# Sparse attention and a ReLU-squared layer: the scores of a batch's two local pairs as one group of 24 matmuls in six PSUM banks

## The chip, the cores and the metric

The kernel runs on one core of a Trainium2 chip. The metric is device time in microseconds (us) of one execution; a figure without further words is the median of several. One execution was also taken by the profiler, and its times are the ones that the lines of the profile show. The engines are named as in the profile: PE (TensorE, matmuls) with PEld (its weight loads), ACT (ScalarE), DVE (VectorE), POOL (GpSimd) and SP (SyncE, here a queue of DMA starts). Each engine takes its instructions in the order in which the program gives them.

## What is computed

Attention with two sparse masks over 8 batches, 8 heads, 576 positions of 64 values, then a two-layer network over the 4608 tokens:

```python
mask_local = (rel >= 0) & (rel < 32)                       # heads 0 to 3
mask_strided = (rel >= 0) & (pos[None, :] % 32 == pos[:, None] % 32)   # heads 4 to 7
attn = softmax(where(mask, q @ k.T / sqrt(64), -1e9))
x = (attn @ v)            # to [8*576, 8*64] = [4608, 512]
h = x @ w_in              # 512 -> 2048
out = relu(h)**2 @ w_out  # 2048 -> 512
```

Inputs and output are float32; the kernel computes with bfloat16 operands.

## The kernel before

**Units.** Heads go in pairs, since two heads of 64 values fill 128 partitions: unit u = 4 b + p is pair p of batch b. Pairs 0 and 1 of a batch are local, pairs 2 and 3 strided. A local query sees only the 31 positions before it, so the scores of a local unit are cut into six blocks of 96 queries against 128 keys. Each block is one matmul per head (line 493): 64 rows of the array, weights from `kT`, moving data from `qT`, 96 columns. The first head of the pair lies in partitions 0 to 63 and the second in 64 to 127 (`row` 0 and 1 in the code), and the matmuls of the two alternate.

**Groups.** The network is the main line of work. It is cut into chunks of 512 tokens (c = 0 to 8). Each chunk has 16 groups of the first layer (line 662: four matmuls of 512 columns into a `ph` bank, then a ReLU on ACT, line 668, then its square on DVE, line 669) and 16 groups of the second layer (line 684: four matmuls; after each fourth group a copy on ACT, line 688, and a store). That gives 288 groups, numbered 0 to 287: group n belongs to chunk n // 32 and is of the first layer where n % 32 < 16. `ph` has two banks, used in turn.

**The plan.** The attention of the batches after the first is woven into these groups by a hand-written table, `PLAN`: "44: S9! D8.0" means that before group 44 the steps S of unit 9 and D of unit 8 are issued. The letters that matter here: T transposes q or k of a unit on PE; S makes the scores of a unit; D (lines 614 to 628) multiplies the exponentials of one head (`.0` or `.1`) with v, six matmuls of 65 columns, and DVE normalises the result; E sends it, by a transposing DMA on SP's queue, to `xt`, the input of the network; Q, C, U and V start loads on POOL's queue; X and Y start transposing DMAs on SP's; s and x are the two halves of the strided pairs' attention; k, B and c are copies that prepare operands.

**Step S from batch 1 on.** It takes four banks from the ring `pt`, two per head, and puts three blocks (288 columns) into each. ACT then takes the exponential of each bank (line 503), and DVE multiplies with the 0/1 mask (line 509), one instruction of 576 columns per head. With "!" the four exponentials are issued at once and the masks of the two heads one and two ticks later; without it the exponentials too are spread over ticks. A tick follows each group: work that was put off with `later(n, ...)` is issued at the n-th tick from there. The square of a group's ReLU is put off by one, so it is issued right behind its own group.

**Banks.** PSUM has eight: two `ph`, five `pt`, one `py`. `bank("pt")` hands out the banks of the ring in order, so each step gets the one that was used longest ago. `py` is last used in chunk 0, that is, before group 32. Step x (lines 544 to 568) takes two banks: `pn` for the sums and `po` for the result; ACT takes the logarithm of `pn` (line 554) and the exponential of that (line 555), and only then DVE multiplies `po` with it into `xt` (line 562, six instructions of 144 columns; for part 2 line 568, four instructions), so `po` stays in use until the last of these.

Of the kernel before, what the change touches and what calls it, by code (L numbers as in the profile page):

```python
# [9 lines left out]
BF16 = mybir.dt.bfloat16  # L10
AF = mybir.ActivationFunctionType
ALU = mybir.AluOpType
# [42 lines left out]
38: T8qv C3k  # L55
39: k20v
40: U3
41: S8! k21v
42: T9qa
44: S9! D8.0  # L60
46: D8.1
47: E8
48: D9.0 Q16k s2.0
49: s2.1
50: Q17q Q16q s2.2 c12kv
51: D9.1 c12qa
52: Q17k c13kv c13qa
54: x2.0 X3q
55: E9 X3k C4k C4q
56: x2.1  # L70
57: T12ka
58: V4 T13qv T12qa
59: T13ka
60: x2.2 B30v
61: B31v
63: U4 S12!
64: X4q
65: D12.0
66: Y17 k30v
67: Y16 D12.1 S13! X4k C5q k31v  # L80
68: C5k
71: s3.0 E12 Q20k Q21q Q20q
72: Q21k s3.1
# [5 lines left out]
83: x3.1  # L89
89: x3.2  # L90
90: k40v
91: S16! k41v
95: U5 D16.0 D16.1
96: S17
97: Y20
99: X5k
100: C6k
# [11 lines left out]
114: k51v  # L109
116: x4.0  # L110
119: x4.1
124: V6
125: x4.2
128: U6 S20!
130: S21
133: D20.0
134: Y24 D20.1 X6k
135: E20 X6q s5.0 C7q Q28k
# [8 lines left out]
150: x5.1 k60v  # L127
152: k61v
153: x5.2
155: S24!  # L130
156: V7
157: U7
161: S25
162: D24.0
165: s6.0 D24.1
166: s6.1
# [7 lines left out]
179: s6.2  # L144
182: x6.1
186: x6.2
188: k70v
189: k71v
191: S28!
192: S29  # L150
197: s7.0
198: D28.0 s7.1
199: D29.0
# [10 lines left out]
def kernel(  # L164
# [9 lines left out]
    nc = tc.nc  # L174
# [40 lines left out]
    def bank(nm):  # L215
        if in_b0[0] and nm == "pt":
            nm = "b0"
        t = banks[nm].pop(0)
        banks[nm].append(t)
        while id(t) in unread:  # L220
            run_due(lambda x: x[1] == unread[id(t)])
        return t
# [16 lines left out]
    mask_bd = singles.tile([128, 1, W3], BF16)  # L239
    str_rows_t = {nm: singles.tile([SR, RW], BF16, name=f"{nm}_t") for nm in "qk"}  # L240
    kTl = [singles.tile([128, 32 + S], BF16, name=f"kTl{i}") for i in range(NV)]
    es = [singles.tile([128, 1280], BF16, name=f"e{i}") for i in range(4)]
    xt = [singles.tile([128, T], BF16, name=f"xt{p}") for p in range(4)]
    w_in_b = singles.tile([128, 4, d_ff], BF16)
    w_out_b = singles.tile([128, 16, d_model], BF16)
# [188 lines left out]
    def later(n, fn, key=None):  # L434
        pending.append((clock[0] + n, key, fn))

    def run_due(test):
        due = [x for x in pending if test(x)]
        for x in due:
            pending.remove(x)  # L440
        for x in sorted(due, key=lambda x: x[0]):
            x[2]()
# [23 lines left out]
    def step_S(u, mode=0):  # L466
        s = st[u]
        qT, kT = s["qT"], s["kT"]
        local = is_local(u)
        w, n = (QL, NL) if local else (SP_, NJ)  # L470
        kn = 128 if local else SP_
        hn = n // 2
        e = es[u % 4]
        s["e"] = e
        pss = [[None, None], [None, None]]
        for half in range(2):
            for row in range(2):
                pss[row][half] = bank("pt")
                if u < 4:
                    bias = bias_l[:, half].rearrange("p t c -> p (t c)") if local \  # L480
                        else bias_s.rearrange("p t c -> p (t c)")
                    nc.tensor.matmul(pss[row][half][0:kn, 0:S // 2], ident[0:kn, 0:kn], bias,
                                     start=True, stop=False, skip_group_check=True)
            for i in range(hn):
                t = half * hn + i
                klo = w * t
                for row in range(2):
                    rows = slice(64 * row, 64 * row + 64)
                    if not local:
                        lhsT, rhs = (a[rows, t // 4, t % 4, :] for a in (kT, qT))  # L490
                    else:
                        lhsT, rhs = kT[rows, klo:klo + kn], qT[rows, w * t:w * (t + 1)]
                    nc.tensor.matmul(pss[row][half][0:kn, w * i:w * (i + 1)], lhsT, rhs,  # L493
                                     start=u > 3, stop=True, skip_group_check=u < 4)

        for row in range(2):
            for half in range(2):
                unread[id(pss[row][half])] = u

        def expo(row, half):  # L500
            del unread[id(pss[row][half])]
            lo = S * row + S // 2 * half
            nc.scalar.activation(e[0:kn, lo:lo + S // 2], pss[row][half][0:kn, 0:S // 2],  # L503
                                 AF.Exp, scale=scale)

        def masks(row):
            x = e[0:kn, S * row:S * (row + 1)].rearrange("p (t c) -> p t c", c=w)
            m = mask_all if local else mask_str.to_broadcast([kn, n, w])
            nc.vector.tensor_tensor(x, x, m, op=ALU.mult)  # L509

        if u < 4:
            for half in range(2):
                for row in range(2):
                    expo(row, half)
            return
        if mode == 1:
            for row in range(2):
                for half in range(2):
                    expo(row, half)
                later(row + 1, lambda row=row: masks(row), u)  # L520
            return
        expo(0, 0)
        later(1, lambda: expo(0, 1), u)
        later(2, lambda: (masks(0), expo(1, 0)), u)
        later(3, lambda: expo(1, 1), u)
        later(4, lambda: masks(1), u)

    def blocks(part):
        return range(NJ * part, min(NJ * (part + 1), NB))

# [81 lines left out]
                rv.rearrange("c (j p) -> c p j", p=SP_), op=ALU.mult)  # L612

    def step_D(u, part):
        run_due(lambda x: x[1] == u)
        s = st[u]
        e = s["e"]
        rhs = s["v"].rearrange("p h t d -> p (h t) d")
        po = bank("pt")[:, 0:NL * (D + 1)].rearrange("p (n d) -> p n d", d=D + 1)
        for n in range(NL):  # L620
            c = QL * (NL * part + n)
            nc.tensor.matmul(po[:, n, :], e[:, c:c + 128], rhs[:, NL * part + n, 0:D + 1], start=True, stop=True)  # L622
        if part == 0:
            s["x"] = xl_pool.tile([QL, 2 * NL, D], BF16, name="x_l")
        x = s["x"].rearrange("p (t h) d -> p h t d", h=2)[:, part]
        rinv = small.tile([128, NL, 1], FP32, name="rinv")
        nc.vector.reciprocal(rinv[0:QL], po[0:QL, :, D:D + 1])
        nc.vector.tensor_tensor(x, po[0:QL, :, 0:D], rinv[0:QL].to_broadcast([QL, NL, D]), op=ALU.mult)  # L628
# [99 lines left out]
    def run_step(word):  # L728
        op, arg = word[0], word[1:]
        if op == "w":  # L730
            warm(int(arg))
        elif op == "c":
            cast_qk_local(int(arg[:-2]), arg[-2], ENG[arg[-1]])
        elif op == "T":
            step_T(int(arg[:-2]), arg[-2], ENG[arg[-1]])
        elif op == "W":
            step_TS(int(arg[0]), arg[1], int(arg[2]), ENG[arg[3]])
        elif op == "S":
            step_S(int(arg.rstrip("!")), int("!" in arg))
        elif op == "N":  # L740
            step_N(int(arg))
        elif op == "O":
            step_O(int(arg))
        elif op in "sx":
            (step_SS if op == "s" else step_XX)(*(int(x) for x in arg.split(".")))
        elif op == "k":
            step_K(int(arg[0]), int(arg[1]), ENG[arg[2]])
        elif op == "m":
            memset_later(arg[:-1], nc.gpsimd if arg[-1] == "g" else nc.vector)
        elif op == "D":  # L750
            u, part = arg.split(".")
            step_D(int(u), int(part))
        elif op == "E":
            step_E(int(arg.rstrip("av")), ENG.get(arg[-1]))
        elif op == "P":
            first_part([int(x) for x in arg])
        elif op == "H":
            shift_v_local(int(arg[:-1]), ENG[arg[-1]])
        elif op == "C":
            load_str_tall(int(arg[:-1]), arg[-1])  # L760
        elif op == "Q":
            load_qk_rows(int(arg[:-1]), arg[-1])
        elif op == "X":
            transpose_str(int(arg[:-1]), arg[-1])
        elif op == "Y":
            transpose_local(int(arg))
        elif op == "V":
            load_v_local_all(int(arg))
        elif op == "U":
            load_v_str(int(arg))  # L770
        elif op == "B":
            spread_v_str(int(arg[0]), int(arg[1]), ENG[arg[2]])
        elif op == "l":
            load_qk_local_sw(int(arg[0]), [int(x) for x in arg[2:].split("+")], arg[1])
        elif op == "r":
            load_str_rows(int(arg[0]), arg[1])
        elif op == "i":
            load_w_in(int(arg))
        elif op == "o":
            load_w_out(int(arg))  # L780
        elif op == "z":
            late_constants()
        else:
            raise ValueError(word)
# [100 lines left out]
    for line in PLAN.strip().splitlines():  # L885
        n, words = line.split(":")
        plan.setdefault(int(n), []).extend(words.split())
    for n, g in enumerate(groups):
        for word in plan.get(n, ()):
            run_step(word)  # L890
        g()
        tick()
# [32 lines left out]
```

## Time and profile before

| | us |
|---|---|
| median of 3 runs | 305.2 (304.89 to 307.47) |
| the profiled execution, whole time | 304.5 |
| its span, first to last instruction | 302.8 |

| engine | busy us | share of the span |
|---|---|---|
| PE | 292.9 | 97% |
| DVE | 179.5 | 59% |
| ACT | 173.2 | 57% |
| POOL | 71.3 | 24% |

| operation | line | mean ns |
|---|---|---|
| matmul of scores, 64 rows, 96 columns, PE | 493 | 205 |
| exponential of 128x288, ACT | 503 | 418 |
| mask of 128x576, DVE | 509 | 453 |
| matmul of D, 65 columns, PE | 622 | 193 |
| ReLU of 128x512, ACT | 668 | 599 |
| square of 128x512, DVE | 669 | 422 |

The times inside the execution are counted from the start of the span. A matmul's duration is its way through the array; matmuls follow each other more closely than that, so how fast PE goes is read from the distance between starts: 216 ns for 512 columns.

### The profile page before, as it was taken

The page shows a single profiled execution, that of the slowest core. Times are in us where ns is not written, and L with a number is a line of the kernel's source. Part 1 is how long each engine was busy: PE and PEld are TensorE (multiplying, and loading weights), DVE is VectorE, ACT ScalarE, POOL GpSimd, SP SyncE. Part 2 cuts the span into 40 slices and gives each one's busy share as a digit, 9 for nine tenths or more (in the row PEclk, how much of TensorE's full clock was granted, in tenths as well). Part 3 has the DMA queues.
Part 4 walks back from the last instruction along what each step waited for, and adds up shares of the span by engine and source line. Part 5 has one row for each costly group of instructions (what it writes and reads, how often), then busy time and mean ns, then how long its engine had stood idle before and what let it go on. Part 6 is the DMA issues. An engine that isn't in the chain of part 4 may idle for free.

```text
span 302.8 us, 5715 instructions
## 1 busy us (share of the span) xinstructions
PE 292.9 (97%) x2143; PEld 146.3 (48%) x2181; DVE 179.5 (59%) x465; ACT 173.2 (57%) x342; POOL 71.3 (24%) x105
## 2 busy tenths in 40 slices
PE   8988999999999999999999999999999999999996
PEld 3543555445555544454454445444454444444444
DVE  5668686888578686585558494676486524104400
ACT  3677853777657744773387446744775447216611
POOL 8734834007213018064300830000000000000000
PEclk9999999999999999999999999999999999999999
DMA  7999999997999999999998999511110110010011
GB/s 149 189 207 196 188 201 187 143 206 124 149 183 159 143 183 151 150 161 119 184 173 153 141 190 153 118 38 67 54 23 19 73 69 0 35 71 35 0 71 70
DMA packets 93643, 37.28 MB, mean 123 GB/s; under 512 B 78956, under 2 KB 87750, under 8 KB 93616
## 3 DMA queue, kind: packets, MB, share of 16 engines
q0 software_dynamic: 54960, 18.82, 62.8%
q1 hardware_dynamic: 38512, 18.03, 30.5%
q8 instruction: 17, 0.28, 0.4%
q14 instruction: 10, 0.08, 0.1%
q10 hardware_dynamic: 144, 0.07, 0.1%
HBM read 38.21 MB, written 9.44 MB: 157 GB/s over the span
## 4 chain that ended last, share of the span: by engine, by line
PE 89%; DVE 3%; issue 2%; DMA 2%; ACT 2%; POOL 0%; DVEq 0%; ACTq 0%; POOLq 0%
PE ph L662 38%; PE ph L684 37%; PE pt L493 2%; DMA w_out_b<-in_k_dram 2%; PE pt L622 2%; PE pt L538 1%; PE pt L552 1%; PE ph L709 1%; PE pt L453 1%; PE pt L549 1%; PE py L684 1%; DVE g_sb L669 1%; DVE xt L562 1%; PE pt L684 1%; ACT r L668 1%
## 5 line engine op out<-in xcount | busy, mean ns | idle before, releaser
L662 PE MATMUL ph<-xt,w_in_b 128*128 128x512 bf16 x548 | 130.5, 379 | 2.3 <-ACT xt L647 1.0
L684 PE MATMUL ph<-w_out_b,g_sb 128*128 128x512 bf16 x513 | 119.7, 379 | 0.8
L668 ACT ACTIVATE r<-ph 128x512 bf16<-128x512 f32 x142 | 84.8, 599 | 35.3 <-PE ph L662 30.2
L669 DVE TENSOR_TENSOR g_sb<-r 128x512 bf16<-128x512 bf16 x144 | 60.4, 422 | 63.8 <-ACT r L668 63.0
L662 PEld LDWEIGHTS <-w_in_b 128*128 128x128 bf16 x576 | 53.0, 97 | 59.7 <-issue 2.3
L684 PEld LDWEIGHTS <-g_sb 128*128 128x128 bf16 x560 | 51.7, 97 | 57.4 <-DVE g_sb L669 0.5
L688 ACT COPY y<-ph 128x512 f32<-128x512 f32 x33 | 19.4, 589 | 53.0 <-PE ph L684 53.0
L562 DVE TENSOR_TENSOR xt<-pt,rv 64x144 bf16<-64x144 f32 x84 | 34.0, 404 | 18.4 <-ACT rv L555 17.3
L503 ACT ACTIVATE e<-pt 128x288 bf16<-128x288 f32 (+1 forms) x68 | 24.0, 417 | 7.7 <-PE pt L493 7.7
L554 ACT ACTIVATE rv<-pt 128x432 f32<-128x432 f32 (+1 forms) x21 | 10.5, 501 | 13.8 <-PE pt L549 13.8
L628 DVE TENSOR_TENSOR x_l<-pt,rinv 96x384 bf16<-96x384 f32 x30 | 16.6, 554 | 1.0
L568 DVE TENSOR_TENSOR xt<-pt,rv 64x270 bf16<-64x270 f32 (+1 forms) x28 | 10.9, 432 | 8.5 <-ACT rv L555 8.4
L509 DVE TENSOR_TENSOR e<-e,mask_all 128x576 bf16<-128x576 bf16 x28 | 12.4, 453 | 3.9 <-ACT e L503 3.6
L539 ACT ACTIVATE e<-pt 128x432 bf16<-128x432 f32 (+1 forms) x21 | 10.4, 497 | 6.6 <-PE pt L538 6.6
L350 POOL DMA_DIRECT2D q_t<-in_q_dram x6 | 3.6, 602 | 44.0 <-DMA qT_s<-q_t 44.0
L419 POOL DMA_DIRECT2D vl<-in_v_dram x7 | 10.1, 1437 | 12.2 <-PE ph L684 6.9
L279 POOL DMA_DIRECT2D k_l<-in_k_dram x16 | 11.9, 751 | 2.9 <-PE pt L552 2.9
L279 POOL DMA_DIRECT2D q_l<-in_q_dram x16 | 11.8, 740 | 2.8 <-DMA k_l<-in_k_dram 1.4
L622 PEld LDWEIGHTS <-e 128*128 128x128 bf16 x192 | 9.1, 97 | 5.8 <-issue 0.4
L555 ACT ACTIVATE rv<-rv 128x432 f32<-128x432 f32 (+1 forms) x21 | 11.2, 533 | 0.7
L622 PE MATMUL pt<-vl,e 128*128 128x65 bf16 x180 | 9.9, 193 | 0.0
L350 POOL DMA_DIRECT2D k_t<-in_k_dram x6 | 3.2, 538 | 25.2 <-DMA kT_s<-k_t 25.2
(130 smaller groups left out, 216.8 us busy)
## 6 DMA issues: line engine op xcount, KB each, us to landing
out_dram<-y SPq DMA_DIRECT2D x35, 256.0 KB, 3.9
vl<-in_v_dram POOLq DMA_DIRECT2D x7, 384.0 KB, 12.4
w_in_b<-in_moe_w_in_dram POOLq DMA_DIRECT2D x4, 512.0 KB, 13.1
w_out_b<-in_moe_w_out_dram POOLq DMA_DIRECT2D x4, 512.0 KB, 13.1
q_t<-in_q_dram POOLq DMA_DIRECT2D x7, 288.0 KB, 6.6
k_t<-in_k_dram POOLq DMA_DIRECT2D x7, 288.0 KB, 5.8
v_st<-in_v_dram POOLq DMA_DIRECT2D x7, 216.0 KB, 8.5
k_l<-in_k_dram POOLq DMA_DIRECT2D x16, 72.0 KB, 7.9
```

The costliest lines, as they stand in the source:

```text
L279: nc.gpsimd.dma_start(out=t[:, :, hh, :], in_=src[b, 2 * p + hh].rearrange("(t p) d -> p t d", p=QL))
L503: nc.scalar.activation(e[0:kn, lo:lo + S // 2], pss[row][half][0:kn, 0:S // 2], AF.Exp, scale=scale)
L509: nc.vector.tensor_tensor(x, x, m, op=ALU.mult)
L555: nc.scalar.activation(rv, rv, AF.Exp, scale=-1.0)
L562: nc.vector.tensor_tensor(to[:, :, NJ * part:NJ * (part + 1), par], of, by, op=ALU.mult)
L622: nc.tensor.matmul(po[:, n, :], e[:, c:c + 128], rhs[:, NL * part + n, 0:D + 1], start=True, stop=True)
L628: nc.vector.tensor_tensor(x, po[0:QL, :, 0:D], rinv[0:QL].to_broadcast([QL, NL, D]), op=ALU.mult)
L662: nc.tensor.matmul(ph, w_in_b[:, kk, 128 * ff:128 * (ff + 1)], xt[kk][:, 512 * c:512 * (c + 1)], start=(kk == order[0]), stop=(kk == order ...
L668: nc.scalar.activation(r, ph, AF.Relu)
L669: later(1, lambda: nc.vector.tensor_tensor(g[:, ff, :], r, r, op=ALU.mult))
L684: nc.tensor.matmul(py, g[:, ff, 128 * j:128 * (j + 1)], w_out_b[:, ff, :], start=(ff == 0), stop=(ff == 15))
L688: nc.scalar.copy(y, py)
```

## The change

From batch 2 on the two steps S of a batch become one step G: `G2` at group 47 stands for `S8!` at 41 and `S9!` at 44; `G3` at 61 for 63 and 67; `G4` at 91 for 91 and 96; `G5` at 122 for 128 and 130; `G6` at 155 for 155 and 161; `G7` at 188 for 191 and 192. G takes six banks, three per head, and puts four blocks (384 columns) of the 12 of a head into each; six exponentials of 384 columns follow, all issued in the step, and the masks of the first head two and of the second head three ticks later. `py` joins the ring `pt` at group 32. The exponentials of both units lie in one tile, first head of both, then second head of both. Around batch 2 some steps of D, E, s and x move by one to five groups, as the diff shows; the positions of the steps E9, x2.1 and x2.2 stay, and those of all D, E, s and x steps of the later batches.

```diff
-41: S8! k21v
+41: k21v
 42: T9qa
-44: S9! D8.0
-46: D8.1
-47: E8
-48: D9.0 Q16k s2.0
-49: s2.1
-50: Q17q Q16q s2.2 c12kv
-51: D9.1 c12qa
-52: Q17k c13kv c13qa
-54: x2.0 X3q
-55: E9 X3k C4k C4q
+47: G2
+48: Q16k
+49: D8.0
+50: Q17q Q16q c12kv D8.1 s2.0
+51: c12qa D9.0 s2.1
+52: Q17k c13kv c13qa E8
+53: s2.2 D9.1
+54: X3q
+55: E9 X3k C4k C4q x2.0
 56: x2.1
...
 60: x2.2 B30v
-61: B31v
-63: U4 S12!
+61: B31v G3
+63: U4
...
-67: Y16 D12.1 S13! X4k C5q k31v
+67: Y16 D12.1 X4k C5q k31v
...
 89: x3.2
 90: k40v
-91: S16! k41v
+91: G4 k41v
 95: U5 D16.0 D16.1
-96: S17
...
 119: x4.1
+122: G5
 124: V6
 125: x4.2
-128: U6 S20!
-130: S21
+128: U6
...
 150: x5.1 k60v
 152: k61v
 153: x5.2
-155: S24!
+155: G6
...
-161: S25
...
 186: x6.2
-188: k70v
+188: G7 k70v
 189: k71v
-191: S28!
-192: S29
...
-    es = [singles.tile([128, 1280], BF16, name=f"e{i}") for i in range(4)]
+    es01 = singles.tile([128, 2560], BF16, name="e01")
+    es = [es01[:, 0:1280], es01[:, 1280:2560]] + [singles.tile([128, 1280], BF16, name=f"e{i}") for i in (2, 3)]
...
+    def step_G(b):
+
+        us = (4 * b, 4 * b + 1)
+        bk = [[bank("pt") for _ in range(3)] for _ in range(2)]
+        for t in range(2 * NL):
+            for row in range(2):
+                s, j = st[us[t // NL]], t % NL
+                rows, c = slice(64 * row, 64 * row + 64), QL * (t % 4)
+                nc.tensor.matmul(bk[row][t // 4][:, c:c + QL], s["kT"][rows, QL * j:QL * j + 128],
+                                 s["qT"][rows, QL * j:QL * (j + 1)], start=True, stop=True)
+        e = es01[:, 0:4 * S].rearrange("p (r c) -> p r c", r=2)
+
+        def masks(row):
+            x = e[:, row].rearrange("p (u t c) -> p u t c", u=2, c=QL)
+            for i in range(2):
+                nc.vector.tensor_tensor(x[:, i], x[:, i], mask_all, op=ALU.mult)
+
+        for row in range(2):
+            for i in range(3):
+                nc.scalar.activation(e[:, row, 4 * QL * i:4 * QL * (i + 1)], bk[row][i][:, 0:4 * QL], AF.Exp, scale=scale)
+            later(row + 2, lambda row=row: masks(row), ("G", b, row))
...
     def step_D(u, part):
-        run_due(lambda x: x[1] == u)
+        run_due(lambda x: x[1] in (u, ("G", u // 4, part)))
...
-        e = s["e"]
+        e = es01[:, 2 * S * part + S * (u % 4):] if u > 7 else es[u % 4][:, S * part:]
...
-            c = QL * (NL * part + n)
+            c = QL * n
...
     for n, g in enumerate(groups):
+        if n == 32:
+            banks["pt"] += banks.pop("py")
         for word in plan.get(n, ()):
             run_step(word)
         g()
```

## The prediction

> **What bounds the kernel.** I read the page first, for the engines and the chain.
>
> ```profile
> PE 292.9 (97%) x2143; PEld 146.3 (48%) x2181; DVE 179.5 (59%) x465; ACT 173.2 (57%) x342; POOL 71.3 (24%) x105
> ...
> PE 89%; DVE 3%; issue 2%; DMA 2%; ACT 2%; POOL 0%; DVEq 0%; ACTq 0%; POOLq 0%
> ```
>
> PE is busy for 97% and makes up 89% of the chain. Then the waits of PE, to see whether it ever stops:
>
> ```profile
> PE ph L662 <- ACT xt L647: 1.0, 1, 1.0
> ...
> PE pt L493 <- ACT e L503: 0.5, 1, 0.5
> ```
>
> These are single waits before 57 us, in batches 0 and 1. Behind that, the starts of the matmuls follow each other at 216 ns with three kinds of exception: distances of about 431 (one record missing between two), two short stops of 0.10 us (at 67.0) and 0.17 us (at 94.7), and the surroundings of the steps S. So from group 32 on the time is a sum of PE's work. What the change takes from PE is won in full, what makes PE wait is lost in full, and ACT and DVE count only where PE waits for them.
>
> **What one group saves.** In order of time, the chain shows a step S between two layers' groups:
>
> ```profile
> 87.97 0.65 PE ph L684 x3
> 88.61 0.36 PE pt L493 x12
> 88.98 0.97 PE ph L684 x4
> 89.94 0.86 PE ph L662 x4
> ```
>
> S takes 0.36 us, and the four matmuls behind it 0.97 instead of 0.86. The distances between starts say why: the last 512-column matmul ahead of S takes 312 ns instead of 216 (96 lost); inside S the two heads' matmuls start 4 ns apart and the next pair 45 ns after; and from the last start to the next layer's matmul it is 135 instead of some 45 (90 lost). Entering and leaving the 64-row matmuls so costs 0.186 us a step. G has the same 24 matmuls as two steps S, with one entry and one exit: six batches x 0.186 = 1.12 us saved. With S9 and S13 out of the first layer the two short stops should go too: 0.27. Together **1.4 us saved**.
>
> The exponentials save nothing on PE's path. On ACT, from rows 128x288 (418 ns), 128x432 (526) and 128x512 (599), one of 384 columns is about 0.49 us; four of 288 take 1.31 together, so back to back they follow at 0.30, those of 384 at about 0.38: 2.4 us for six against 2.6 for eight. Masks: four of 576 columns, as before.
>
> **What G2 adds: masks behind a square.** G2 is issued before group 47, the last of the first layer. This is how the same queue looked at S8:
>
> ```profile
> 64.85 0.43 PE L493 MATMUL pt<-qT,kTl 64*128 64x96 bf16 x12
> 64.96 0.60 ACT L668 ACTIVATE r<-ph 128x512 bf16<-128x512 f32 x1 [0.27 <-PE ph L662]
> 65.45 1.31 ACT L503 ACTIVATE e<-pt 128x288 bf16<-128x288 f32 x4
> ...
> 66.61 0.65 ACT L668 ACTIVATE r<-ph 128x512 bf16<-128x512 f32 x1
> ...
> 66.74 0.46 DVE L509 TENSOR_TENSOR e<-e,mask_all 128x576 bf16<-128x576 bf16 x1
> ```
>
> The ReLU of the group before comes first, the exponentials 0.60 us after S has started, and the next ReLU behind them all. With G2: six exponentials end at 0.60 + 5 x 0.38 + 0.49 = 2.99 us from G's start; the ReLU of group 47 is queued behind them and ends at 3.5; its square on DVE ends at 3.9. That square was put off by one tick, the first masks by two, so on DVE they stand **behind** it: done at 4.3 and 4.7. D8.0 is issued before group 49, which PE reaches after G (0.63) and two groups (0.86 each), at 2.36. Its first five matmuls need the first mask, the sixth reads 32 columns of unit 9 and needs the second: it is through at 4.80 instead of 2.54. PE loses 2.3 us, everything behind D8.0 with it. Then the masks of the second head are issued after group 49, behind D8.0's own work on DVE (reciprocal 0.18, product 0.55, ending near 5.8), and end at 6.2 and 6.6; D8.1, before group 50, is reached at 5.66 and could be through at 5.8; it is at 6.65, another 0.85. **3.1 us**. D9.0 and D9.1 find their masks done. In G3 to G7, all beside the second layer, no ReLU stands between, and their D steps come four to eleven groups later: nothing.
>
> **What six banks add: G waits for the step x before it.** The ring hands out banks by age, and with six banks G needs all six, the last two steps' included. The third bank of row 1, written from the ninth pair on (0.36 us after G's start), is the one handed out last. Before G3, G4, G5, G6 and G7 that is `po` of x2.2, x3.2, x4.1, x5.2 and x6.2. S with four banks of five left just that bank alone. From the timeline around x5.2 and S24:
>
> ```profile
> 175.97 0.30 PE L549 MATMUL pt<-e,ones_bd 128*128 128x324 bf16 x1
> ...
> 176.78 0.47 ACT L555 ACTIVATE rv<-rv 128x324 f32<-128x324 f32 x1
> ...
> 178.09 0.43 PE L493 MATMUL pt<-qT,kTl 64*128 64x96 bf16 x12
> ...
> 178.91 1.59 DVE L568 TENSOR_TENSOR xt<-pt,rv 64x270 bf16<-64x270 f32 x4
> ```
>
> DVE, busy with x5.1 and with k60v and k61v, reads `po` of x5.2 until 180.50. G6 stands in S24's place and wants that bank at 178.09 + 0.36 = 178.45: 2.1 us of stop. The others in the same way, the last read of `po` in line 562 or 568 against the ninth pair, with 0.05 for the signal: G3 (group 61 starts at 86.71; x2.2's `po` read until 88.79) 1.6; G4 (S16's place, 116.21; until 116.98) 0.45; G5 (group 122 at 146.1; until 146.93) 0.5; G7 (group 188 at 210.2; until 210.87) 0.3. Sum **4.95 us**. G2 finds its banks free, T9qa being five groups back.
>
> What moves in batch 2: s2.0 to s2.2 and D8, D9 go with PE, whose work in them is the same. x2.0 comes one group later, directly ahead of x2.1; their twelve instructions on DVE (5.0 us in the trace, without a gap) then end just as x2.2 wants a bank of x2.1, a stop of up to 0.3 us that G3's larger stop contains. E8 is sent five groups later, just ahead of X3q and E9 on SP's queue. E9 landed 8.5 us after its start, at 88.5, and group 64 read it from 89.94. One more transposing DMA before it costs 1.2 to 2.9 us of SP, but group 64 also comes 1.6 later by G3's stop: I take nothing, at most 2 us. k30v waits for X3k, which landed at 89.4 and is used at 93.0: hidden likewise.
>
> **Sum.** 3.1 + 4.95 - 1.4 = +6.65 us against the profiled execution's 304.5 (span 302.8 and 1.7 around it), so 311.1 for one like it. That execution lies 0.7 under the median of the runs; on the median, 305.2 + 6.65 = **311.8**.
>
> Unknown here: how soon PE goes on after a stop for DVE (0.02 to 0.15 us each, seven times: under 0.8 in all, I take 0.05), and the end of six exponentials (five distances of 0.30 as for 288 columns, or of 0.53, a whole one of 432: -0.4 to +0.75 on D8.0, I take 0.38, nearer the first since the four overlap).
>
> **Rivals.**
> - *Switches only.* PE would never wait: 305.2 - 1.4 = 303.8, not slower. It turns on `po` being read out by 0.36 us after G's start, and the masks ahead of the square. For it: G7 and G4 miss the first by under half a microsecond. Against: at G6 and G3 DVE is over 1.5 us late by the rows, and the order on DVE is fixed by the ticks. 0.05.
> - *Only one of the two waits.* The banks alone: 305.2 + 4.95 - 1.4 = 308.7. The masks alone (if a bank were free earlier than its last reader): 306.9. 0.05 each.
> - *No switch saved*, if changing banks within G costs PE as much as leaving it: 1.1 more, 312.9. Nothing in S, which changes banks once in the middle at the same 45 ns, speaks for it. 0.05.
> - *E9 late.* The network's chunk 2 waits for `xt`: up to 2 more, 312 to 314. 0.10; the DMA engines are busy nine tenths in that stretch, and landing took 2.5 to 11.3 us.
> - *The clock.* The trace has PE slow once: its first ten matmuls, from 1.27 to 5.51 us, start 427 ns apart, then 216. Stops of 1.2 us (at 18.7 and 28.4) did not bring this back. If D8.0's 2.3 us of stop did, 4.2 us at half pace would cost 2.1: 313.8, twice (G6 as well) 315.9. 0.05.
>
> The Trainium skill speaks against the change here: the page "TensorE: Matmul & The Clock Gate", section "HAM oscillation — how this bites in real kernels", says that idle stretches above some 3.4 us let the clock fall to half. By that rule the sum stays, since the longest stop above is shorter, but only by about a microsecond; no stop of that length is in this trace.
>
> **Numbers.** The forecast, both waits as sized, has 0.65. Range 308.2 to 314.5: down to the banks alone, with the wait and the distance of exponentials at their lower ends; up to E9 late or one fall of the clock. Left out are switches only, masks alone, and the far ends of the clock and of E9: under 2 in 10. A measurement of this kernel tells about 1% (3 us) from no change. Faster by more than that: 0.02 (1.4 us is all there is to win). Within: switches only, masks alone and a small part of banks alone: 0.11. Slower: 0.87.
>
> **What would show it.** Right: in the waits of PE, line 622 waits for DVE's mask once for about 2 us and once for under 1, at group 49 and 50; the G matmuls wait for DVE at lines 562 or 568 in five places, longest in batch 6. ACT has 36 exponentials of 128x384 at 0.49 us. The 312 and 135 ns distances appear six times instead of twelve behind 60 us. Wrong: no idle PE in these places; or new stops elsewhere, at group 64 (line 662, waiting for a DMA) above all.

## The result and the profile after

| | before | after |
|---|---|---|
| median, us | 305.2 | 312.65 (312.43 to 312.94, four executions) |
| the profiled execution, whole time | 304.5 | 312.94 |
| its span | 302.8 | 311.2 |

The changed kernel is slower: ratio 1.0249, 95% interval 1.0224 to 1.0275. The span grew by 8.4 us.

First the page of the changed kernel, busy times and the chain by engine. (Its lines are numbered anew: 680 and 702 are the matmuls of the two layers, 686 the ReLU, 687 the square, 532 the scores of G, 543 its exponentials, 539 its masks, 640 the matmuls of D, 580 and 586 DVE's reads of `po`.)

```profile
PE 296.8 (95%) x2181; PEld 147.4 (47%) x2181; DVE 181.4 (58%) x465; ACT 173.7 (56%) x330; POOL 71.2 (23%) x105
...
PE 82%; DVE 8%; ACT 5%; issue 2%; DMA 2%; POOL 0%; DVEq 0%; ACTq 0%; POOLq 0%
```

PE's part of the chain fell from 89 to 82%, and DVE's and ACT's rose from 5 to 13%: over long stretches the end is now set by what PE waits for. The waits of PE (engine and line that waited, for whom; us in total, times, longest) name the places:

```profile
PE pt L640 <- DVE e L539: 1.9, 1, 1.9
PE py L532 <- DVE xt L586: 1.9, 1, 1.9
PE pt L532 <- DVE xt L586: 1.7, 3, 1.1
...
PE py L640 <- DVE e L539: 0.5, 1, 0.5
PE pt L532 <- DVE xt L580: 0.5, 1, 0.5
```

D waits twice for the masks, G five times for a bank that DVE is still reading. This view leaves out the time of a matmul's way through the array. The distances between the starts of matmuls, less the distance where nothing waits, give each stop in full. Beside the forecast:

| stop | forecast, us | in the trace, us |
|---|---|---|
| D8.0 | 2.3 | 2.24 |
| D8.1 | 0.85 | 0.76 |
| G3 (with x2.2's own 0.34) | 1.6 | 1.63 |
| G4 | 0.45 | 0.42 |
| G5 | 0.5 | 0.61 |
| G6 | 2.1 | 2.01 |
| G7 | 0.3 | 0.43 |
| entries and exits saved | -1.12 | -1.12 |
| two short stops gone | -0.27 | -0.27 |
| the clock | 0 | 1.6 |
| sum | 6.65 (from rounded parts) | 8.3 |

All terms but one came within 0.15 us. The timeline of batch 2 shows both the queue that was forecast and the clock, which the sum had at nothing:

```profile
70.43 0.34 PE L532 MATMUL pt<-qT,kTl 64*128 64x96 bf16 x8
70.53 0.60 ACT L686 ACTIVATE r<-ph 128x512 bf16<-128x512 f32 x1 [0.27 <-PE ph L680]
...
71.03 0.48 ACT L543 ACTIVATE e<-pt 128x384 bf16<-128x384 f32 x1
...
71.77 1.66 ACT L543 ACTIVATE e<-pt 128x384 bf16<-128x384 f32 x4
...
73.25 0.67 ACT L686 ACTIVATE r<-ph 128x512 bf16<-128x512 f32 x1
73.95 0.42 DVE L687 TENSOR_TENSOR g_sb<-r 128x512 bf16<-128x512 bf16 x1 [2.36 <-ACT r L686]
...
74.29 0.82 DVE L539 TENSOR_TENSOR e<-e,mask_all 128x576 bf16<-128x576 bf16 x2
74.89 0.48 PE L640 MATMUL pt<-vl,e 128*128 128x65 bf16 x6 [1.94 <-DVE e L539]
...
76.11 0.81 DVE L539 TENSOR_TENSOR e<-e,mask_all 128x576 bf16<-128x576 bf16 x2
76.70 0.51 PE L640 MATMUL py<-vl,e 128*128 128x65 bf16 x6 [0.46 <-DVE e L539]
...
77.39 1.88 PE L702 MATMUL ph<-w_out_b,g_sb 128*128 128x512 bf16 x4
```

DVE was idle for 2.36 us ahead of the square. The exponentials of the first head had ended at 72.28, 1.7 us before the square started at 73.95, but their masks stood behind it in the queue. And in the last line four matmuls take 1.88 us where four take 1.03 elsewhere. That is the clock. Three stretches of 3.41 us by time (busy us and instructions of PE, PEld, DVE, ACT, POOL, then the granted clock, the DMA share and GB/s):

```profile
73.44:76.85 3.41, 1.50 (x15) 0.73 (x15) 2.57 (x8) 0.48 (x1) 2.89 (x5) 1.00 1.02 163
76.85:80.27 3.42, 3.42 (x34) 1.94 (x32) 2.06 (x7) 1.51 (x3) 1.45 (x2) 0.50 1.77 125
80.27:83.68 3.41, 3.41 (x28) 1.76 (x27) 1.79 (x6) 1.92 (x4) 0.73 (x1) 1.00 1.22 147
```

For one stretch PE had half its clock, right behind one in which it had worked 1.50 of 3.41 us. The missing 1.91 us are 1.45 of D8.0's stop, which had begun before the stretch, and 0.46 of D8.1's. The stop of G6, for the last bank of x5.2, in the timeline:

```profile
182.32 0.30 PE L567 MATMUL pt<-e,ones_bd 128*128 128x324 bf16 x1
...
184.44 0.55 PE L532 MATMUL pt<-qT,kTl 64*128 64x96 bf16 x17
...
185.25 1.56 DVE L586 TENSOR_TENSOR xt<-py,rv 64x270 bf16<-64x270 f32 x4
...
186.86 0.20 PE L532 MATMUL py<-qT,kTl 64*128 64x96 bf16 x1 [1.86 <-DVE xt L586]
```

Seventeen of G's matmuls go, the ninth pair's second one stands until DVE's last read of `po` has ended at 186.81, and the rest follows.

### The profile page after: what moved, and what is told of

Its sections match the earlier page's. It is cut to its first block, busy times and chain, and to the rows that moved or that the text cites. A ratio compares the mean times of both kernels' runs of the same rounds, so it can differ in the third digit from the quotient of the medians.

```text
span 311.2 us, 5730 instructions
## 1 busy us (share of the span) xinstructions
PE 296.8 (95%) x2181; PEld 147.4 (47%) x2181; DVE 181.4 (58%) x465; ACT 173.7 (56%) x330; POOL 71.2 (23%) x105
## 4 chain that ended last, share of the span: by engine, by line
PE 82%; DVE 8%; ACT 5%; issue 2%; DMA 2%; POOL 0%; DVEq 0%; ACTq 0%; POOLq 0%
PE ph L680 37%; PE ph L702 32%; DVE xt L580 3%; DVE xt L586 2%; DMA w_out_b<-in_k_dram 2%; PE pt L640 1%; PE pt L556 1%; PE pt L449 1%; PE ph L727 1%; ACT rv L573 1%; ACT r L686 1%; ACT rv L572 1%; PE py L702 1%; PE pt L567 1%; DVE g_sb L687 1%
## 5 line engine op out<-in xcount | busy, mean ns | idle before, releaser
L702 PE MATMUL ph<-w_out_b,g_sb 128*128 128x512 bf16 x528 | 122.6, 381 | 0.0
L680 PEld LDWEIGHTS <-w_in_b 128*128 128x128 bf16 x576 | 53.7, 98 | 60.5 <-issue 1.7
L580 DVE TENSOR_TENSOR xt<-pt,rv 64x144 bf16<-64x144 f32 x72 | 29.1, 404 | 15.2 <-ACT rv L573 14.3
L543 ACT ACTIVATE e<-pt 128x384 bf16<-128x384 f32 x30 | 12.8, 501 | 5.7 <-PE pt L532 4.2
L572 ACT ACTIVATE rv<-pt 128x432 f32<-128x432 f32 (+1 forms) x18 | 9.0, 502 | 11.9 <-PE pt L567 11.9
L646 DVE TENSOR_TENSOR x_l<-pt,rinv 96x384 bf16<-96x384 f32 x24 | 13.3, 554 | 0.8
L586 DVE TENSOR_TENSOR xt<-pt,rv 64x270 bf16<-64x270 f32 (+1 forms) x24 | 9.3, 431 | 6.3 <-ACT rv L573 6.2
L539 DVE TENSOR_TENSOR e<-e,mask_all 128x576 bf16<-128x576 bf16 x24 | 9.9, 455 | 1.6 <-ACT e L543 1.4
L640 PE MATMUL pt<-vl,e 128*128 128x65 bf16 x144 | 8.4, 195 | 1.9 <-DVE e L539 1.9
```

Source lines behind the costliest of these rows:

```text
L543: nc.scalar.activation(e[:, row, 4 * QL * i:4 * QL * (i + 1)], bk[row][i][:, 0:4 * QL], AF.Exp, scale=scale)
L580: nc.vector.tensor_tensor(to[:, :, NJ * part:NJ * (part + 1), par], of, by, op=ALU.mult)
L586: nc.vector.tensor_tensor(t, of[:, g:, :, lo:lo + k], by[:, g:, :, lo:lo + k], op=ALU.mult)
L680: nc.tensor.matmul(ph, w_in_b[:, kk, 128 * ff:128 * (ff + 1)], xt[kk][:, 512 * c:512 * (c + 1)], start=(kk == order[0]), stop=(kk == order ...
L702: nc.tensor.matmul(py, g[:, ff, 128 * j:128 * (j + 1)], w_out_b[:, ff, :], start=(ff == 0), stop=(ff == 15))
```

## Experiments

The theory at this point: three separate losses (masks queued behind a square; G in need of the step x's last bank; the clock behind a long stop), and one gain of 1.4 us. Each run below is compared with runs of the kernel before on the same chip. To read the medians: executions of one kernel differ, though not by that alone, by whether the clock fell in them, which the mean clock of each tells (0.999 to 1.000 without, 0.994 or 0.995 with one such stretch).

### The masks ahead of the square

```diff
-            later(row + 2, lambda row=row: masks(row), ("G", b, row))
+            later(row + (1 if b == 2 else 2), lambda row=row: masks(row), ("G", b, row))
```

> Edit: for batch 2 alone, the masks of the first head are put off by one tick instead of two, those of the second by two instead of three, so that DVE gets the first ones ahead of the square of group 47. Theory (the stop of D8.0 is the masks' place behind a square whose ReLU waits for six exponentials): the masks of the first head are done about 2.8 us after G2's start, D8.0's stop falls from 2.24 to some 0.35 us, D8.1's goes from 0.76 to some 0.9, and the clock stays at 1.00 since PE no longer stands for 2 us: 312.65 - 1.75 - 1.6 = 309.3. Rival (D8.0 waits for the exponentials themselves, or for the second head's): the stop stays at about 2 us and the time at 312.6.

Measured: 311.2 us (kernel before 304.76), ratio 1.0191 (1.0156 to 1.0227). The timeline of this kernel around D8:

```profile
71.70 1.66 ACT L543 ACTIVATE e<-pt 128x384 bf16<-128x384 f32 x4
...
71.86 0.84 DVE L539 TENSOR_TENSOR e<-e,mask_all 128x576 bf16<-128x576 bf16 x2 [0.34 <-ACT e L543]
...
72.71 0.34 PE L640 MATMUL pt<-vl,e 128*128 128x65 bf16 x6
...
73.88 0.43 DVE L687 TENSOR_TENSOR g_sb<-r 128x512 bf16<-128x512 bf16 x1 [1.18 <-ACT r L686]
74.22 0.82 DVE L539 TENSOR_TENSOR e<-e,mask_all 128x576 bf16<-128x576 bf16 x2
74.82 0.48 PE L640 MATMUL py<-vl,e 128*128 128x65 bf16 x6 [0.90 <-DVE e L539]
```

The first masks now run while the exponentials of the second head are still going, and D8.0 does not stop at all; the second ones are the ones behind the square, and D8.1 stops 1.2 us, where 0.9 was expected. Of 3.0 us in the two places 1.2 are left. That shows the cause of D8.0's stop. The time fell less than expected, and the clock says why: it stayed at 1.00 in batch 2, as expected, but in the profiled execution it fell at G6 instead, where it had not fallen before:

```profile
180.07:183.48 3.41, 1.56 (x25) 0.75 (x25) 3.27 (x11) 0.98 (x3) 0.00 (x0) 1.00 1.72 174
183.48:186.89 3.41, 3.41 (x15) 1.34 (x15) 1.68 (x4) 2.22 (x5) 0.00 (x0) 0.50 0.51 90
```

Four executions: 309.84 with a mean clock of 1.000, and 311.17, 311.22 and 311.30 with 0.994. So the one without a fall is within 0.6 of the 309.3 expected, and by these four a fall costs 1.4.

### G3 to G7 moved back

```diff
-61: B31v G3
+61: B31v
-63: U4
-65: D12.0
+63: U4 G3
-67: Y16 D12.1 X4k C5q k31v
+67: Y16 D12.0 X4k C5q k31v
+69: D12.1
-91: G4 k41v
-95: U5 D16.0 D16.1
-97: Y20
+91: k41v
+92: G4
+95: U5
+96: D16.0
+97: Y20 D16.1
-122: G5
+123: G5
-155: G6
+158: G6
-188: G7 k70v
-189: k71v
+188: k70v
+189: G7 k71v
```

> Edit: G3 to G7 are moved back to 63, 92, 123, 158 and 189, where the step x before them has been read out; D12.0, D12.1, D16.0 and D16.1 move back with them to 67, 69, 96 and 97. G2 stays as it is. Theory (G waits for the last bank of the step x before it): the five stops, 5.05 us in all, go, and the rest stays: 312.65 - 5.05 = 307.6, with the clock's stretch in batch 2 still there. Rival (G waits for its six banks whatever stands before it, or the stops come back at other steps because DVE is late as a whole): less than half of that is won, 310 or more.

Measured: 308.75 us, ratio 1.0118 (1.0086 to 1.015). No matmul of G waits any longer in the trace, so the five stops did come from the step x before. The median is 1.1 above the expected: group 65 now stops 0.96 us (the next run shows at what). One execution without a fall of the clock took 307.3; the profiled one, 308.86, has it at 76.8, as the changed kernel has.

### Both, with D8 moved back

The two edits above, and:

```diff
-49: D8.0
-50: Q17q Q16q c12kv D8.1 s2.0
+50: Q17q Q16q c12kv D8.0 s2.0
-52: Q17k c13kv c13qa E8
-53: s2.2 D9.1
-54: X3q
+52: Q17k c13kv c13qa D8.1
+53: s2.2 D9.1
+54: E8 X3q
```

> Edit: the two edits of the other runs together, and D8.0, D8.1 and E8 moved back to 50, 52 and 54. It keeps all of the change: one group of 24 matmuls, six banks, exponentials of 384 columns. Theory (what PE lost is only waits of placement, what it gains are the six entries and exits and two short stops): no stop of PE over 0.2 us behind group 47, clock 1.00, and 305.2 - 1.4 = 303.8. Rival (the merging saves nothing, or the six banks cost elsewhere): 305 or more.

Measured: 304.74 us against 304.76, ratio 1.0 (0.9973 to 1.0028). This is 7.9 us under the changed kernel and the time of the kernel before, with all of the merging kept. The gain that was expected (303.8) is missing, and two stops are left, 0.35 us at x2.2 (for a bank of x2.1, which DVE reads until then) and 0.96 at group 65. The timeline for the second:

```profile
90.57 1.28 ACT L544 ACTIVATE e<-pt 128x384 bf16<-128x384 f32 x3
...
91.68 0.65 ACT L707 COPY y<-ph 128x512 f32<-128x512 f32 x1
...
92.38 0.81 PE L681 MATMUL ph<-xt,w_in_b 128*128 128x512 bf16 x3 [0.80 <-ACT y L707]
```

Group 65 needs the `ph` bank that the copy of group 63 empties, and on ACT that copy stands behind G3's six exponentials. It is the pattern of D8.0 on another engine: the block of exponentials delays what is queued behind it. The next run moves both and both go.

### The gain by itself

On the kernel of the last run:

```diff
-53: s2.2 D9.1
-54: E8 X3q
-55: E9 X3k C4k C4q x2.0
-56: x2.1
+53: s2.2 D9.1 x2.0
+54: E8 X3q x2.1
+55: E9 X3k C4k C4q
-59: T13ka
-60: x2.2 B30v
+59: T13ka x2.2 B30v
-63: U4 G3
+62: G3
+63: U4
+65: D12.0
-67: Y16 D12.0 X4k C5q k31v
-69: D12.1
+67: Y16 D12.1 X4k C5q k31v
...
+                def expo(row=row, i=i):
+                    nc.scalar.activation(...)
+                later(2, expo) if (b, row, i) == (3, 1, 2) else expo()
```

> Edit on the kernel with both edits: x2.0, x2.1 and x2.2 move forward to 53, 54 and 59 and G3 to 62, D12.0 and D12.1 return to 65 and 67, and the last exponential of G3 is put off by two ticks, behind the copy of group 63. In the run before, two stops were left in batch 2 and 3: x2.2 waited 0.35 us for a bank of x2.1, and group 65 waited 0.96 us for the copy of group 63, which stood behind six exponentials. Theory: both go, no stop over 0.2 us is left, and 304.74 - 1.3 = 303.4, 0.4 to 0.5% under the kernel before (304.76): just the entries and exits saved. Rival (something else ate what the merging saves, or it saves nothing): 304.5 or more.

Measured: 303.19 us against 304.68, ratio 0.9943 (0.9926 to 0.996). Its executions lie between 303.04 and 303.31. This is faster than both kernels. The page of this kernel:

```profile
PE 290.8 (96%) x2143; PEld 146.2 (48%) x2181; DVE 180.3 (60%) x465; ACT 173.3 (57%) x330; POOL 72.3 (24%) x105
...
PE 89%; DVE 3%; issue 2%; DMA 2%; ACT 2%; POOL 0%; DVEq 0%; ACTq 0%; POOLq 0%
```

The chain is back to the shares of before, and behind 60 us no wait of PE is over 0.3 us. Of the 1.5 us in the medians (1.2 in the spans of the two profiled executions) the starts of the scores show 1.1: there are six distances of 311 or 312 ns at the entries and six exits, where the kernel before has eleven of 311 or 312, one of 126 (entered from the short matmuls of D), and twelve exits of 135. The two short stops of the kernel before, 0.27 in all, are gone, and one of 0.09 is new.

The same edit undone in part: inside G, the layer's group behind it is issued between the matmuls of the two units (the lines that hand this group to G are left out).

```diff
         for t in range(2 * NL):
+            if t == NL:
+                between.pop()()
             for row in range(2):
```

> Edit on the kernel of 303.19: inside each G the layer's group that follows it is issued between the matmuls of the first and those of the second unit, so that the 64-row matmuls are entered and left twice a batch again; banks, exponentials and masks stay. Theory (what the merging wins is one entry and one exit a batch, 96 and 90 ns): six times 0.186 comes back, 303.19 + 1.1 = 304.3, and the trace has twelve distances of 312 and twelve of 135 ns behind 60 us. Rival (the 1.5 us under the kernel before come from the placement of x2.0 to x2.2 and the sixth bank): 303.2 to 303.5.

Measured: 306.44 us, ratio 1.0062 (1.0048 to 1.0075). The twelve entries of 311 or 312 and the twelve exits of 135 are there, 1.1 us of the 3.25 lost. The rest was not expected, and the time fits neither the theory (304.3) nor the rival (303.2 to 303.5): the second unit's scores come 1.1 us later, the first exponential in batch 2 starts 1.93 us behind G's start instead of 0.60, and PE now stops at D8.1 (0.15), D12.1 (0.18), x4.1 (0.14) and, longest, at two first-layer groups. The waits of this kernel name the holders of the `ph` banks and of `xt`:

```profile
PE ph L686 <- DVE xt L592: 0.7, 2, 0.4
PE ph L686 <- ACT y L712: 0.6, 1, 0.6
```

The starts give 1.8 us for all of these; about 0.3 of the 3.25 is not accounted for. So the size of the gain is read from the distances rather than from this run's time, which does not show it by itself.

The sixth bank alone, on the kernel before:

```diff
     for n, g in enumerate(groups):
+        if n == 32:
+            banks["pt"] += banks.pop("py")
```

> Edit on the kernel before: py joins the ring at group 32, nothing else. Theory (a sixth bank alone neither wins nor costs, since no step there waits for a bank behind 60 us): 304.7, within 0.3 us of the kernel before. Rival (the sixth bank is what helps, or the longer ring costs): over 0.5 us of difference.

Measured: 304.89 us against 304.65, ratio 1.002 (1.0001 to 1.0038). It wins nothing. The profiled execution, 304.54 with a span of 302.8, is as long as that of the kernel before. The interval allows a loss of up to 1.2 us, and two of the ten executions, 306.28 and 307.27, have the clock's fall (0.994). So the sixth bank does not explain the gain.

### The clock

Matmuls as a filler in D8.0's and D8.1's stops:

```diff
+    FILL = {(8, 0): 10, (8, 1): 3}
+
     def step_D(u, part):
...
+        if (u, part) in FILL:
+            pf = banks["pt"][0]
+            for _ in range(FILL[u, part]):
+                nc.tensor.matmul(pf, w_in_b[:, 0, 0:128], w_in_b[:, 0, 0:512], start=True, stop=True)
         po = bank("pt")[:, 0:NL * (D + 1)].rearrange("p (n d) -> p n d", d=D + 1)
```

> Edit: ten matmuls of 512 columns on weights that are there, their result unused, are issued ahead of D8.0 and three ahead of D8.1, so that PE works through both stops; nothing else changes. This adds work and takes none away. Theory (the clock fell because PE stood still): the clock stays at 1.00 in this stretch, D8.0 and D8.1 end where they did (ten matmuls are 2.16 us, three 0.65), and 1.6 us are won: 311.0. Rival (the clock falls for another reason, the change from 64-row to 128-row matmuls or the load of the other engines): the stretch at 0.7 stays and the time is 312.6 or more.

Measured: median 313.22, ratio 1.0258 (1.0225 to 1.0292): the rival's number. But the profiled execution took 311.4 at a mean clock of 1.000, and its timeline shows what the theory said: D8.0 and D8.1 run when they did, with PE at work ahead of them.

```profile
72.80 2.32 PE L642 MATMUL pt<-w_in_b 128*128 128x512 bf16 x9
...
74.96 0.43 PE L646 MATMUL pt<-vl,e 128*128 128x65 bf16 x6
...
77.25 1.02 PE L708 MATMUL ph<-w_out_b,g_sb 128*128 128x512 bf16 x4
```

The three others took 313.19 to 313.48 at 0.995: the clock fell in them after all, in a place that no profile shows. The longest stop left is G6's 2.0 us, and the run with the masks ahead has the fall just there; that it is the place here too is inferred. So filling the stop kept the clock up in batch 2 in the execution that was traced, and did not make the kernel faster by the median.

What decides it? In each of the three profiles with a fall inside the kernel, the trace's record of the clock has it for 3413 ns, and it starts a whole number of such windows after the clock first rose (21, 21 and 52 of 3413.3 ns). So windows were laid over the traces by that first rise, and PE's work in the window that holds a stop was read off. For the fall with G later, the two windows are these:

```profile
73.35:76.76 3.41, 1.60 (x15) 0.81 (x17) 2.73 (x8) 0.32 (x1) 2.73 (x4) 1.00 1.26 146
76.76:80.18 3.42, 3.42 (x30) 1.95 (x30) 2.06 (x6) 1.67 (x3) 1.45 (x2) 0.50 1.71 116
```

The longest stops without a fall come next. First the filler's G6:

```profile
183.59:187.01 3.42, 1.69 (x14) 0.88 (x14) 2.61 (x8) 1.93 (x6) 0.00 (x0) 1.00 1.10 187
187.01:190.42 3.41, 3.36 (x17) 1.55 (x16) 0.78 (x2) 1.08 (x3) 0.00 (x0) 1.00 0.24 85
```

Then the G6 of the run that puts it at 154, which comes below:

```profile
180.68:184.09 3.41, 1.78 (x14) 0.98 (x15) 2.63 (x7) 1.60 (x4) 0.00 (x0) 1.00 1.69 169
184.09:187.51 3.42, 3.42 (x18) 1.57 (x16) 0.53 (x2) 0.62 (x2) 0.00 (x0) 1.00 0.30 94
```

And the changed kernel's own stop at G6, which was as long as in the run with the masks ahead but lay across a window's border:

```profile
182.67:186.08 3.41, 2.33 (x30) 1.05 (x26) 3.28 (x11) 1.77 (x4) 0.04 (x1) 1.00 1.79 147
186.08:189.50 3.42, 2.64 (x19) 1.27 (x18) 2.48 (x6) 2.12 (x5) 0.00 (x0) 1.00 0.88 145
```

Before a fall PE had worked 1.50 us (the changed kernel), 1.56 (masks ahead) and 1.60 (G later); with 1.69 and 1.78 it did not fall. From the rise of the clock to the last matmuls, every other whole window of the eleven traces holds more than 2.0 us of work, and none is followed by a fall. At the kernel's end the first window with less than 1 us of work (0 to 0.87) is followed by a fall in each of the eleven. So in these traces the border lies between 1.60 and 1.69 us, somewhat under half a window, by ends of matmuls that the profile models.

To test that by a stop of chosen length, G6 alone was put at two other places of the kernel with both edits:

```diff
-158: G6
+154: G6
```

> Edit on the kernel with both edits: G6 alone moves from 158 to 154, one group behind x5.2. It waits for the last bank of x5.2, by the trace of the changed kernel 2.0 us at 155, so 2.9 us here. Theory (the clock is judged in windows of 3.41 us that run on by themselves, and falls to half for one window when PE stood in more than 1.3 to 1.7 us of the one before): a stop of 2.9 us falls nearly always so far into one window that the clock falls, costing 1.7: mean clock 0.994 in most executions, 304.74 + 2.9 + 1.7 = 309.3. Rival (only a stop longer than a whole window of 3.4 us lets the clock fall, and batch 2 had another cause): clock 1.00 and 307.6 in all executions.

Measured: 309.19 us, ratio 1.015 (1.0122 to 1.0178). The three timed executions, 309.08 to 310.87, all have a mean clock of 0.994. In the profiled one (308.64) the clock stayed at 1.00: its stop of 2.87 us was cut in two by a window's border, leaving the 1.78 us of work shown above. A wait for a transposing DMA in G5 (1.2 us in the view of the waits) is in its time too, so that it comes near the 309.3 for another reason than the expected one. The rival, that only a stop longer than a whole window counts, expected 1.00 in all executions and does not hold. That the three fell at G6 is inferred from their clock; none of them was traced.

```diff
-156: V7
+156: V7 G6
-158: G6
```

> Edit on the kernel with both edits: G6 alone moves from 158 to 156. Its wait for the last bank of x5.2 is then one group shorter than at 155, 1.15 us. Theory of the windows: too short for the clock, which stays at 1.00 in all executions, and 304.74 + 1.15 = 305.9. Rival (each stop of PE in G has its price in clock): 0.994 in some executions, 307.6 there. Rival of the bank wait (the stop is not the distance to x5.2): less than 0.5 or more than 2 us of stop.

Measured: 305.8 us, ratio 1.0029 (1.0012 to 1.0046). The stop is 1.17 us in the trace, where 1.15 was expected, so the bank wait is the distance to x5.2 and nothing else. Nine of ten executions have a clock of 0.999 or 1.000 and lie between 305.42 and 306.11; one, 307.35, has 0.994. No profile shows where it fell in that one. One of 17 executions of the kernel before (306.45), two of ten with the sixth bank alone and two of twelve with both edits (306.8 at 0.994, 308.28 at 0.989) have falls too. So falls also occur where the traced executions have no stop of 2 us; what brings them there stays open.

## Why the prediction was right

The time was 312.65 for a forecast of 311.8, inside the range. That the two lie only 0.85 us apart is in part luck: from one profiled execution to the other the time grew by 8.4 us and not by 6.65. The forecast started from a median of 305.2, and later groups of 15 to 17 executions of the kernel before have medians of 304.65 to 304.76, so a base half a microsecond too high covered a part of the term that was missing. By its steps:

- **What bounds the kernel** held. PE's chain was dense, and each stop came into the time in full: the table's rows add up to 8.3 of the 8.4 us by which the span grew, and with these seven stops moved away the median was 7.9 us lower, the clock's part included.
- **What one group saves** held in size: 96 and 90 ns six times. In the changed kernel it is covered by the stops; with those gone the kernel is 1.5 us under the one before.
- **Masks behind a square** held, queue by queue: 2.24 and 0.76 us for 2.3 and 0.85, and the run that only turned the two round on DVE took D8.0's stop away.
- **G waits for the step x before it** held: 5.10 us for 4.95, in the five places, with G6 and G3 the longest as forecast; G6 at 156 instead of 155 has one group less of it.
- **What moves in batch 2** held: x2.2 stopped 0.34 us for x2.1's bank, where up to 0.3 was forecast as a part of G3's stop. No group 64 waits for E9.
- **The sum** lacked one term. The rival "the clock" was given 0.05, and all four executions have a clock of 0.995. The step that failed is the reasoning beside it, that the stops of 1.2 us in batch 0 had done nothing and that 2.3 us would rarely do more: D8.0's stop and D8.1's fell into one window together and left 1.50 us of work in it. The price was close: 2.1 forecast for one fall; 1.6 in the trace, since it lasts one window of 3.41 us at half pace and not the 4.2 us of the start.

The page "TensorE: Matmul & The Clock Gate" of the Trainium skill has the window, in "What's actually happening": 3413 ns, running on by itself; three profiles here agree with it to the nanosecond. Its rule of thumb in "HAM oscillation — how this bites in real kernels" is to leave no idle gaps of PE above some 3.4 us. As a limit that is too wide here: a stop of 2.0 us (G6, masks ahead) was enough where one window held most of it, and so were stops of 2.24 and 0.76 us close together.

## What to carry to other kernels

Where one engine is dense, judge a merged step not by its instructions but by its needs: the resource that it takes last (here the youngest bank of a full ring), and the work that is queued behind its block on in-order engines (here a ReLU, its square, and a copy that empties a bank). The seven waits here were worked out from the trace of before to within 0.15 us by comparing when PE arrives with when the last reader ends. Then move the step by that much: the same merging that cost 2.5% won 0.6% when it was placed by those two rules. It took two rounds, because moving steps made a new wait (0.96 us for a copy behind the exponentials) that had not been forecast.

## What was not expected of the hardware

The granted clock of TensorE fell to half for one window of 3413 ns after a window in which PE had worked 1.50 to 1.60 us, and did not after 1.69 and 1.78 us. So a stop of 2 us may or may not cost another 1.6 us (the changed kernel's trace), depending on where a window's border lies in it: with the masks ahead, the same kernel took 309.84 us in one execution and 311.2 to 311.3 in three. With the filler the executions with and without a fall lie 1.8 to 2.1 us apart, more than one window at half pace (1.71) can cost; the rest is not explained.
